# A gated recurrence, worked in units of two chunks of 128 tokens in place of one, ahead of a routed expert layer

## The chip, the cores and the metric

One core of a Trainium2 chip runs the kernel. The metric is the device time of one execution in microseconds, as the median of several runs.

## The reference, cut to what matters

Eight heads of 48 run a gated outer-product recurrence over 768 steps in each of 4 batches; the result, as 3072 tokens of 384, goes through a layer of 8 experts, one expert for each token.

```python
f = 1.0 / (1.0 + np.exp(-f_logit))            # (4, 8, 768, 48)
for t in range(S):
    state = f[:, :, t, :, None] * state + np.einsum('bhd,bhe->bhde', k[:, :, t], v[:, :, t])
    y[:, :, t] = np.einsum('bhd,bhde->bhe', q[:, :, t], state)
x = y.transpose(0, 2, 1, 3).reshape(3072, 384)
logits = x @ w_gate                           # (3072, 8)
expert_idx = np.argmax(logits, axis=1)
gate_w = softmax(logits)[arange, expert_idx]
y[i] = gate_w[i] * (relu(x[i] @ w1[e]) @ w2[e])   # e = expert_idx[i], F = 1024
```

## The kernel before, in words

There are two stages. The first computes the recurrence in 24 chunks of 128 tokens of one batch (`steps`: two batches alternate, then the other two), and routes each token's row to its expert's region of a table `xs` in memory. The second goes over the table in 31 tiles of 128 rows, each with one expert's weights, and scatters the results to the output (from line 513). Between them VectorE works out which tile has which expert, and SyncE writes a tile of padding behind each region (lines 464 to 507). The change is in the first stage alone.

A chunk holds 8 heads as 4 pairs; a head of a pair has 48 of the partitions 0 to 63 or of 64 to 127. So a tile of q, k or f is 128 partitions by 4 pairs by 128 tokens, 512 elements wide. `load` (line 201) fetches it in halves of 96 KB, and v in one transfer, into 5 slots whose unused partitions were filled once (line 194). `prep` (line 213) makes the running product r of 1 + exp(-f) by an Exp, a "plus one" on GpSimd and four scans on VectorE, one for each pair (line 222), capped at 1e19; the decay is exp(-ln r) (lines 224 and 225: Ln and Exp, each with a load of its function table); q is multiplied by the decay, k by r.

`score` (line 231) has the products k by q for each head (16 matmul instructions, as each f32 product takes two), the transposes of k (line 240), a masked copy of the scores by VectorE (line 243) and a copy of the transposed keys by ScalarE (line 245). `rows` (line 270) adds up the rows: "within" (line 274, scores by v) and "before" (line 285, the old state by q), and copies them out (line 294). `update` (line 248) makes the new state: the state products (line 253), a sum and a multiplication by the last decay on VectorE (lines 264 and 265). `gate` (line 297) transposes the rows (line 300, 4 transposes), multiplies them by the gate weights (line 305, 8 thin instructions of 8 columns, with a 128 x 128 weight load each), and copies both out. After each fourth chunk `route` (line 144) chooses the expert, counts by two products with constants (lines 157 and 158), works out each row's position by small VectorE operations, and sends the four chunks by indirect DMAs from GpSimd (line 132).

The loop (line 329) issues these in an order in which the rows of a chunk come one step after its scores. Tile's own scheduler orders the instructions on each engine by priority and readiness. All loads, and one expert's second weights `w2r` in every second step (line 334), go through SyncE's queue. At the end a sum over `rend` (lines 382 to 391) says whether any product reached the cap, in which case another, slow form of the recurrence would run; the data here don't reach it.

## Time and profile before

| | us |
|---|---|
| median of 3 runs (687.83 to 692.0) | 688.04 |
| the profiled execution | 696.35 |
| its span | 694.4 |
| busy: TensorE matmul, its weight loads | 574.7, 457.8 |
| busy: VectorE, ScalarE, GpSimd | 184.4, 164.0, 116.9 |
| mean granted TensorE clock | 0.837 |

The span is the time from the first to the last profiled instruction. Busy times are sums over instructions that don't wait; matmuls are pipelined, so a busy TensorE is not one at its peak. [...] Of all transfers, 100.70 MB in 64164 packets, the mean rate over the span is 145 GB/s.

### The profile page before, as it was taken

What the parts mean: (1) busy time and instruction counts of PE and PEld (TensorE: products, weight loads), DVE (VectorE), ACT (ScalarE), POOL (GpSimd) and SP (SyncE); (2) the same over time, 40 slices, a digit from 0 to 9 for tenths busy, and PEclk for the clock granted to TensorE, in tenths of its full rate; (3) what the DMA queues carried; (4) which work ended last, traced back from release to release, by engine and by line L of the source; (5) the groups of instructions that cost most, each with busy time, mean ns of one, the idle gap of its engine ahead of it and who ended that gap; (6) DMA issues with size and microseconds to landing.
All of it is one profiled execution on the core that took longest, in us unless ns stands there. A gap on an engine that the chain in (4) does not pass through costs nothing.

```text
span 694.4 us, 10369 instructions
## 1 busy us (share of the span) xinstructions
PE 574.7 (83%) x3895; PEld 457.8 (66%) x3895; DVE 184.4 (27%) x504; ACT 164.0 (24%) x231; POOL 116.9 (17%) x185
## 2 busy tenths in 40 slices
PE   0788897696897699506999999999899999999995
PEld 0677776575775577405867777777678677776864
DVE  3555352343253363310111111111111111111120
ACT  4765444536345544101000000000000000000000
POOL 8224213114113123100101010101001010000001
PEclk9988655755565755657999999999999999999998
DMA  7697555653623001055554545453444545363500
GB/s 203 161 268 217 187 133 167 174 158 108 176 62 98 28 1 48 24 194 236 162 182 150 183 131 203 135 206 117 161 169 147 192 134 203 115 215 118 204 32 1
DMA packets 64164, 100.70 MB, mean 145 GB/s; under 512 B 5726, under 2 KB 46721, under 8 KB 64112
## 3 DMA queue, kind: packets, MB, share of 16 engines
q1 hardware_dynamic: 59744, 89.79, 40.8%
q0 software_dynamic: 3520, 9.64, 3.7%
q8 instruction: 33, 0.54, 0.3%
q10 hardware_dynamic: 848, 0.57, 0.3%
q14 instruction: 19, 0.16, 0.1%
HBM read 88.50 MB, written 12.85 MB: 146 GB/s over the span
## 4 chain that ended last, share of the span: by engine, by line
issue 48%; POOL 4%; PE 2%; SPq 1%; DMA 1%; POOLq 0%; DVE 0%
POOL out_dram L132 4%; PE hps L536 1%; DMA xrow<-xs 1%; PE yps L550 1%; SPq L467 1%; SPq L468 0%; POOLq L132 0%; POOLq L594 0%; SPq L517 0%; SPq L516 0%; SPq L519 0%; DVE ysb L554 0%; SPq L521 0%; DVE dst L529 0%
## 5 line engine op out<-in xcount | busy, mean ns | idle before, releaser
L536 PE MATMUL hps<-xT,w1t 128*128 128x128 f32 x1488 | 174.2, 277 | 13.4 <-DVE xT L527 7.6
L536 PEld LDWEIGHTS hps<-xT,w1t 128*128 128x128 f32 x1488 | 171.1, 193 | 21.3 <-DVE xT L527 11.2
L550 PE MATMUL yps<-w2r,hT 128*128 x496 | 171.0, 493 | 13.5 <-DVE hT L546 13.5
L550 PEld LDWEIGHTS yps<-w2r,hT 128*128 128x128 f32 x496 | 90.9, 191 | 77.4 <-DVE hT L546 24.4
L544 ACT ACTIVATE hT<-hps 128x512 f32<-128x512 f32 x31 | 18.5, 597 | 337.4 <-PE hps L536 337.4
L132 POOL DMA_INDIRECT out_dram<-ysb,dst x31 | 30.3, 978 | 361.8 <-DVE ysb L554 326.7
L529 DVE CAST dst<-xrow 128x1 int32<-128x1 f32 x31 | 4.8, 154 | 213.5 <-DMA out_dram<-ysb,dst 193.4
L240 PE MATMUL kp<-fpack,k 128*128 128x128 f32 x96 | 23.6, 389 | 44.4 <-POOL k L228 44.4
L274 PE MATMUL yt<-at,v 128*64 128x128 f32 x384 | 51.2, 382 | 3.8 <-DVE at L243 3.7
L235 PE MATMUL s<-q,k 48*128 48x128 f32 x384 | 48.5, 405 | 3.0 <-DVE q L227 2.9
L240 PEld LDWEIGHTS kp<-fpack,k 128*128 128x128 f32 x96 | 16.0, 203 | 48.9 <-POOL k L228 47.4
L235 PEld LDWEIGHTS s<-q,k 48*128 48x128 f32 x384 | 40.1, 289 | 9.1 <-DVE q L227 5.4
L554 DVE TENSOR_SCALAR ysb<-yps,xrow 128x384 f32<-128x384 f32 x31 | 19.2, 618 | 101.4 <-PE yps L550 101.4
L274 PEld LDWEIGHTS yt<-at,v 128*64 128x64 f32 x384 | 36.4, 193 | 11.4 <-DVE at L243 6.4
L222 DVE TENSOR_TENSOR_SCAN r<-z,fpack 128x128 f32<-128x128 f32 x96 | 35.0, 419 | 24.9 <-POOL z L219 22.9
L243 DVE COPY_PREDICATED at<-mpack,s 128x512 f32<-128x512 uint8 x48 | 33.1, 724 | 30.7 <-PE s L235 30.7
L305 PEld LDWEIGHTS lp<-wg,ys 128*128 128x128 f32 x192 | 33.5, 262 | 4.2 <-issue 2.2
L285 PE MATMUL yt<-q,state 48*48 48x128 f32 x320 | 34.9, 354 | 0.0
L305 PE MATMUL lp<-wg,ys 128*128 128x8 f32 x192 | 33.8, 304 | 0.9 <-ACT ys L294 0.7
L132 POOL DMA_INDIRECT xs<-xr,posi x24 | 24.5, 1022 | 59.3 <-DVE posi L170 34.1
L219 POOL TENSOR_SCALAR z<-z 128x512 f32<-128x512 f32 x24 | 15.7, 655 | 93.2 <-ACT z L218 93.1
L224 ACT ACT_TABLE_LOAD x24 | 30.8, 1283 | 0.4
(86 smaller groups left out, 417.3 us busy)
## 6 DMA issues: line engine op xcount, KB each, us to landing
w1t<-in_moe_w_dram SPq DMA_DIRECT2D x31, 1536.0 KB
w2r<-in_moe_w_dram SPq DMA_DIRECT2D x8, 1536.0 KB
xrow<-xs SPq DMA_DIRECT2D x31, 200.0 KB
v<-in_v_dram SPq DMA_DIRECT2D x24, 256.0 KB
k<-in_kT_dram SPq DMA_DIRECT2D x48, 96.0 KB
f<-in_fT_dram SPq DMA_DIRECT2D x48, 96.0 KB
q<-in_qT_dram SPq DMA_DIRECT2D x48, 96.0 KB
xs<-pad SPq DMA_DIRECT2D x8, 200.0 KB
```

Source lines behind the costliest of these rows:

```text
L132: ins = nc.gpsimd.indirect_dma_start(out=dst, out_offset=bass.IndirectOffsetOnAxis(ap=idx, axis=0), in_=src, in_offset=None, bounds_check= ...
L222: nc.vector.tensor_tensor_scan(r[:, p], z[:, p], const("top"), 1.0, OP.mult, OP.min)
L224: nc.scalar.activation(dec, r, AF.Ln)
L235: nc.tensor.matmul(ps[a][:, p], lhsT=k[r, p], rhs=q[r, p], start=True, stop=True)
L240: nc.tensor.transpose(kp[:, p], k[:, p], ident)
L243: nc.vector.copy_predicated(at[:, :, a], _bc(causal, 1, HP), ps[a])
L274: nc.tensor.matmul(yt[DP * a : DP * a + DP, p], lhsT=vt[:, 2 * p + a], rhs=at[:, p, a], start=p == 0, stop=c == 0, skip_group_check=True,)
L285: nc.tensor.matmul(yt[r, p], lhsT=old[r, p], rhs=q[r, p], start=False, stop=True, skip_group_check=True,)
L305: nc.tensor.matmul(lp, lhsT=ys[:, p], rhs=wg[:, p], start=p == 0, stop=p == HP - 1)
L536: nc.tensor.matmul(hp[:, f, :], lhsT=w1t[:, j, o : o + 128], rhs=xT[:, j, :], start=j == 0, stop=j == KD - 1,)
L550: nc.tensor.matmul(yp, lhsT=hT[:, f, :], rhs=w2r[:, ds(er, 1), f, :], start=f == 0, stop=f == NF - 1)
L554: nc.vector.tensor_scalar(ysb, yp, xt[:, GATE : GATE + 1], None, op0=OP.mult)
```

## The change

A unit is one chunk of two batches: 8 pairs, 1024 elements wide (`SEG` pairs of `C` tokens). The host lays q, k, f and v out by units with the unused partitions filled, so that a unit is loaded by four transfers. Each segment of f gets one more column in front (`CR`), which sets the running product back to 1 (`RESET` there, and 1 in the cap's first column), so that one scan runs over all 8 pairs. All of f, r-logarithm and decay lie in f's own tile. The state's multiplication by the last decay goes to GpSimd. The transposes of the rows and the gate products become one product per pair with a constant of 104 columns: 96 that select the two heads' rows and 8 of gate weights; VectorE adds the four pairs' gate parts (`reduce_sum`). `route` is cut into five calls, of the same operations. The order of the instructions on each of five engines is the order in which the program issues them (`manual_schedule`): pass n of the loop has the scores of unit n, "within" and "before" of unit n - 1, rows and route of unit n - 2, and the front parts of units n + 1 and n + 2. Routes come after units 1, 3, 5, 7 and 9 for two units, and after 10 and 11 for one. The loads of unit n + 3 end the pass; three buffers hold a unit's inputs.

```diff
+NU = B // 2 * NC
+SEG = 2 * HP
+CR = C + 1
+RESET = -30.0
...
+GROUPS = [[u, u + 1] for u in range(0, NU - 2, 2)] + [[NU - 2], [NU - 1]]
+XW = 2 * D + E
...
+    sel = np.zeros((128, HP, XW))
+    for a in range(2):
+        sel[DP * a + np.arange(D), :, D * a + np.arange(D)] = 1.0
+    f["rows"] = sel.reshape(128, HP * XW)
...
+    wx = const("rows").rearrange("p (h w) -> p h w", w=XW)
+    halves = [(a, slice(DP * a, DP * a + D)) for a in range(2)]
+    for a, r in halves:
+        nc.scalar.dma_start(
+            wx[r, :, 2 * D : XW],
+            moe_w_gate.rearrange("(p two d) e -> two d p e", two=2, d=D)[a],
+        )
...
+    class Route:
...
+        def choose(self):
...
+        def count(self, rp):
+            self.rp = rp
+            nc.tensor.matmul(rp[:, 0], lhsT=const("tri"), rhs=self.oh, start=True, stop=True)
+            nc.tensor.matmul(rp[:, 1], lhsT=const("ones"), rhs=self.oh, start=True, stop=True)
+        def place(self):
...
+        def weigh(self):
+            nc.scalar.activation(self.ex, self.ex, AF.Exp)
+        def send(self):
...
+        ld = st.enter_context(tc.tile_pool(name="ld", bufs=3))
...
+        cap = wk.tile([128, SEG, CR], F32, name="cap", bufs=1)
+        nc.vector.memset(cap, RTOP)
+        nc.vector.memset(cap[:, :, 0:1], 1.0)
...
+        def load(u, *names):
+            x = units[u]
+            for n in names:
+                src = {"q": qu, "k": ku, "f": fu, "v": vu}[n]
+                if n == "v":
+                    x[n] = ld.tile([128, 2, H, DP], F32, name=n)
+                else:
+                    x[n] = ld.tile([128, SEG, CR if n == "f" else C], F32, name=n)
+                nc.sync.dma_start(x[n], src[u])
+        def growth(u):
+            f = units[u]["f"]
+            nc.scalar.activation(f, f, AF.Exp, scale=-1.0)
+            nc.gpsimd.tensor_scalar(f, f, 1.0, 1.0, op0=OP.add, op1=OP.mult)
+        def product(u):
+            x = units[u]
+            x["r"] = wk.tile([128, SEG, CR], F32, name="r", bufs=1)
+            nc.vector.tensor_tensor_scan(
+                x["r"].rearrange("p s c -> p (s c)"),
+                x["f"].rearrange("p s c -> p (s c)"),
+                cap.rearrange("p s c -> p (s c)"),
+                1.0,
+                OP.mult,
+                OP.min,
+            )
+        def by_r(u):
+            x = units[u]
+            nc.gpsimd.tensor_tensor(x["k"], x["k"], x["r"][:, :, 1:CR], op=OP.mult)
+            nc.gpsimd.tensor_copy(rend[:, u], x["r"][:, :, C])
+        def log_r(u):
+            x = units[u]
+            nc.scalar.activation(x["f"][:, :, 1:CR], x["r"][:, :, 1:CR], AF.Ln)
+        def decay(u):
+            x = units[u]
+            x["dec"] = x["f"][:, :, 1:CR]
+            nc.scalar.activation(x["dec"], x["dec"], AF.Exp, scale=-1.0)
+        def by_decay(u):
+            x = units[u]
+            nc.vector.tensor_tensor(x["q"], x["q"], x["dec"], op=OP.mult)
+        def heads():
+            return [(p, h, slice(DP * h, DP * h + DP)) for p in range(HP) for h in range(2)]
+        def score(u):
+            x = units[u]
+            x["at"] = scores[u % 2]
+            for a in range(2):
+                ps = pss.tile([128, 2, HP, C], F32, name="s")
+                for p, h, r in heads():
+                    s = HP * a + p
+                    nc.tensor.matmul(
+                        ps[:, h, p], lhsT=x["k"][r, s], rhs=x["q"][r, s], start=True, stop=True
                     )
+                nc.vector.copy_predicated(
+                    x["at"][:, a].rearrange("p h s c -> p (h s) c"),
+                    _bc(causal, 1, SEG),
+                    ps.rearrange("p h s c -> p (h s) c"),
+                )
+        def keys(u):
+            x = units[u]
+            x["kn"] = wk.tile([128, SEG, C], F32, name="kn", bufs=1)
             for a in range(2):
+                kp = pst.tile([128, HP, C], F32, name="kp", **tr)
                 for p in range(HP):
+                    nc.tensor.transpose(kp[:, p], x["k"][:, HP * a + p], ident)
+                nc.scalar.copy(x["kn"][:, HP * a : HP * a + HP], kp)
+        def within(u, a):
+            x = units[u]
+            if a == 0:
+                x["yt"] = psy.tile([128, 2, HP, C], F32, name="yt")
+            for p, h, r in heads():
+                nc.tensor.matmul(
+                    x["yt"][r, a, p],
+                    lhsT=x["v"][:, a, 2 * p + h],
+                    rhs=x["at"][:, a, h, p],
+                    start=p == 0,
+                    stop=x["old"] is None,
+                    skip_group_check=True,
+                )
+        def before(u):
+            x = units[u]
+            if x["old"] is None:
+                return
+            for t in range(2):
+                for p in range(HP):
+                    for a in range(2):
+                        h = a ^ t
+                        r = slice(DP * h, DP * h + D)
                         nc.tensor.matmul(
+                            x["yt"][r, a, p],
+                            lhsT=x["old"][r, HP * a + p],
+                            rhs=x["q"][r, HP * a + p],
                             start=False,
                             stop=True,
                             skip_group_check=True,
                         )
+        def added(u):
+            x = units[u]
+            x["dp"] = pst.tile([128, SEG, D], F32, name="dp", **tr)
+            for a in range(2):
+                for p, h, r in heads():
+                    s = HP * a + p
+                    nc.tensor.matmul(
+                        x["dp"][r, s],
+                        lhsT=x["kn"][:, s, r],
+                        rhs=x["v"][:, a, 2 * p + h, 0:D],
+                        start=s == 0,
+                        stop=True,
+                        skip_group_check=True,
+                    )
+        def update(u):
+            x = units[u]
+            new = wk.tile([128, SEG, D], F32, name="state", bufs=4)
+            last = x["dec"][:, :, C - 1 : C].to_broadcast([128, SEG, D])
+            if x["old"] is None:
+                nc.vector.tensor_copy(new, x["dp"])
+            else:
+                nc.vector.tensor_tensor(new, x["dp"], x["old"], op=OP.add)
+            nc.gpsimd.tensor_tensor(new, new, last, op=OP.mult)
+            states[u % 2] = new
+        def settle(u):
+            x = units[u]
+            x["ys"] = wk.tile([128, 2, HP, C], F32, name="ys", bufs=1)
+            for a in range(2):
+                nc.scalar.copy(x["ys"][:, a], x["yt"][:, a])
...
+        def rows(u):
+            x = units[u]
+            g = next(g for g in GROUPS if u in g)
+            if u == g[0]:
+                n = 2 * len(g)
+                group["xr"] = wk.tile([128, n, ROW], F32, tag="xr", name="xr")
+                group["lg"] = wk.tile([128, n, E], F32, tag="lg", name="lg")
+                nc.gpsimd.memset(group["xr"][:, :, USED:ROW], 0.0)
+            for a in range(2):
+                j = 2 * (u - g[0]) + a
+                xp = pst.tile([128, HP, XW], F32, name="xp", **tr)
+                for p in range(HP):
+                    nc.tensor.matmul(
+                        xp[:, p], lhsT=x["ys"][:, a, p], rhs=wx[:, p], start=True, stop=True
+                    )
+                nc.scalar.copy(
+                    group["xr"][:, j, 0:DM].rearrange("p (h w) -> p h w", h=HP),
+                    xp[:, :, 0 : 2 * D],
                 )
+                nc.vector.reduce_sum(
+                    group["lg"][:, j],
+                    xp[:, :, 2 * D : XW].rearrange("p h e -> p e h"),
+                    axis=AX_X,
                 )
...
+        st.enter_context(tc.manual_schedule(engines=ordered))
+        for u in range(3):
+            load(u, *"fkqv")
+        growth(0)
+        product(0)
+        by_r(0)
+        log_r(0)
+        decay(0)
+        by_decay(0)
+        growth(1)
+        product(1)
+        for n in range(NU + 2):
+            here, back, last = n, n - 1, n - 2
+            rt = None
+            if here < NU:
+                units[here]["old"] = states[here % 2]
+                score(here)
+            if 0 <= last:
+                settle(last)
+            if n + 1 < NU:
+                by_r(n + 1)
+                log_r(n + 1)
+            if 0 <= last:
+                rt = rows(last)
+                if rt:
+                    rt.choose()
+            if here < NU:
+                keys(here)
+            if 0 <= back < NU:
+                within(back, 0)
+            if rt:
+                rt.count(pst.tile([128, 2, rt.n, E], F32, name="rp", **tr))
+            if 0 <= back < NU:
+                within(back, 1)
+            if n + 1 < NU:
+                decay(n + 1)
+                by_decay(n + 1)
+            if rt:
+                rt.place()
+            if here < NU:
+                if here // 2 < NC - 1:
+                    added(here)
+            if n + 2 < NU:
+                growth(n + 2)
+            if rt:
+                rt.weigh()
+            if here < NU and here // 2 < NC - 1:
+                update(here)
+            if rt:
+                rt.send()
+            if n + 2 < NU:
+                product(n + 2)
+            if 0 <= back < NU:
+                before(back)
+            if n + 3 < NU:
+                load(n + 3, *"fkqv")
+            if 1 <= n <= E:
+                e = n - 1
                 nc.sync.dma_start(w2r[:, e], moe_w2[e].rearrange("(f p) d -> p f d", p=128))
...
+    fu = np.full((NU, 128, SEG, CR), RESET, v.dtype)
+    fu[..., 1:] = unit(inputs["f_logit"], 30.0)
```

The fallback and the call of `route` in it use the five calls; nothing from line 464 on is changed.

## Rows read from the trace of the kernel before

**Rows 1.** The page's 40 slices: TensorE's granted clock in tenths.

```profile
PEclk9988655755565755657999999999999999999998
```

**Rows 2.** Stretches of time; the first line names the columns.

```profile
core 0: us, PE busy (x) PEld busy (x) DVE busy (x) ACT busy (x) POOL busy (x), PEclk, DMA share, GB/s
18.70:291.40 272.70, 224.06 (x1811) 185.31 (x1810) 113.32 (x349) 135.68 (x190) 66.24 (x95) 0.65 0.43 125
128.00:132.00 4.00, 4.00 (x58) 3.65 (x54) 1.51 (x3) 0.71 (x2) 0.00 (x0) 1.00 0.67 168
132.00:136.00 4.00, 0.22 (x5) 0.00 (x0) 1.37 (x4) 2.85 (x4) 1.04 (x3) 1.00 1.06 373
136.00:140.00 4.00, 2.64 (x16) 2.24 (x18) 0.69 (x1) 3.21 (x5) 1.59 (x2) 0.60 0.86 178
248.00:260.00 12.00, 12.00 (x79) 9.62 (x80) 6.88 (x31) 4.96 (x9) 2.71 (x4) 0.50 0.01 2
310.00:320.00 10.00, 2.72 (x12) 2.38 (x12) 0.87 (x3) 0.00 (x0) 0.00 (x0) 0.50 1.01 400
```

**Rows 3.** Timeline of TensorE at the full clock: start, length.

```profile
59.12 0.67 PE L253 MATMUL dp<-v,kn 128*64 128x48 f32 x16
61.21 0.63 PE L240 MATMUL kp<-fpack,k 128*128 128x128 f32 x4
...
127.53 1.16 PE L235 MATMUL s<-q,k 48*128 48x128 f32 x16
128.63 0.65 PE L300 MATMUL xtp<-fpack,ys 128*128 128x128 f32 x4
129.12 0.96 PE L305 MATMUL lp<-wg,ys 128*128 128x8 f32 x8
130.00 1.21 PE L274 MATMUL yt<-at,v 128*64 128x128 f32 x16
131.14 1.08 PE L285 MATMUL yt<-q,state 48*48 48x128 f32 x16
```

**Rows 4.** Timeline of TensorE at half the clock.

```profile
265.90 2.08 PE L235 MATMUL s<-q,k 48*128 48x128 f32 x16
```

**Rows 5.** Groups of the first stage: busy us, mean ns, idle before.

```profile
L222 DVE TENSOR_TENSOR_SCAN r<-z,fpack 128x128 f32<-128x128 f32 x96 | 35.0, 419 | 24.9 <-POOL z L219 22.9 <-issue 1.9
L243 DVE COPY_PREDICATED at<-mpack,s 128x512 f32<-128x512 uint8 x48 | 33.1, 724 | 30.7 <-PE s L235 30.7
L224 ACT ACT_TABLE_LOAD x24 | 30.8, 1283 | 0.4
L228 POOL TENSOR_TENSOR k<-k,r 128x512 f32<-128x512 f32 x24 | 30.6, 1274 | 0.0
L132 POOL DMA_INDIRECT xs<-xr,posi x24 | 24.5, 1022 | 59.3 <-DVE posi L170 34.1 <-DVE place L160 19.4 <-issue 5.2
L227 DVE TENSOR_TENSOR q<-q,dec 128x512 f32<-128x512 f32 x24 | 17.5, 731 | 46.2 <-ACT dec L225 46.2
L219 POOL TENSOR_SCALAR z<-z 128x512 f32<-128x512 f32 x24 | 15.7, 655 | 93.2 <-ACT z L218 93.1
L224 ACT ACTIVATE dec<-r 128x512 f32<-128x512 f32 x24 | 15.1, 630 | 24.3 <-DVE r L222 24.1
L265 DVE TENSOR_TENSOR state<-state,dec 128x192 f32<-128x192 f32 x16 | 10.3, 645 | 0.3
```

**Rows 6.** Groups of the same view, narrow operations.

```profile
L173 ACT ACTIVATE ex<-ex 128x32 f32<-128x32 f32 x6 | 1.4, 231 | 3.0 <-DVE ex L172 3.0
L153 DVE TENSOR_TENSOR eq<-lg,mx 128x32 f32<-128x32 f32 x6 | 1.1, 192 | 0.2
```

**Rows 7.** Timeline of VectorE and GpSimd: a state product beside GpSimd's product.

```profile
197.14 1.27 POOL L228 TENSOR_TENSOR k<-k,r 128x512 f32<-128x512 f32 x1
197.20 1.41 DVE L265 TENSOR_TENSOR state<-state,dec 128x192 f32<-128x192 f32 x1
```

**Rows 8.** Timeline of VectorE: the first reader of the packed constants.

```profile
6.15 0.23 DVE L129 COPY base<-fpack 128x8 f32<-128x8 f32 x1 [3.13 <-DMA fpack<-c_fpack]
```

**Rows 9.** Timeline of VectorE: the last routing positions.

```profile
291.19 0.17 DVE L170 CAST posi<-pos 128x4 int32<-128x4 f32 x1
```

More of the change, by code (lines that the diff above doesn't have):

```diff
@@ L87 @@
     vT: bass.AP,
-    v: bass.AP,
+    qu: bass.AP,
+    ku: bass.AP,
+    fu: bass.AP,
+    vu: bass.AP,
     moe_w_gate: bass.AP,
@@ L123 @@
     nc.scalar.dma_start(xs[DUMMY : DUMMY + C], pad)
-    halves = [(a, slice(DP * a, DP * a + D)) for a in range(2)]
-    for a, r in halves:
-        nc.scalar.dma_start(
-            wg[r], moe_w_gate.rearrange("(p two d) e -> two d p e", two=2, d=D)[a]
-        )
     nc.vector.tensor_copy(base[:, 0], const("first"))
@@ L182 @@
+    ordered = {getattr(mybir.EngineType, n) for n in ENGINES}
     with ExitStack() as st:
-        ld = st.enter_context(tc.tile_pool(name="ld", bufs=1))
+        ld = st.enter_context(tc.tile_pool(name="ld", bufs=3))
         wk = st.enter_context(tc.tile_pool(name="wk", bufs=2))
@@ L197 @@
+        nc.vector.memset(cap, RTOP)
+        nc.vector.memset(cap[:, :, 0:1], 1.0)
+        scores = [wk.tile([128, 2, 2, HP, C], F32, name=f"at{i}", bufs=1) for i in range(2)]
         for t in scores:
             nc.vector.memset(t, 0.0)
-        srcs = {"q": qT, "k": kT, "f": fT}
-        def load(n, b, c):
-            cols = slice(c * C, c * C + C)
-            for x in "fkq":
-                for a, r in halves:
-                    nc.sync.dma_start(
-                        slots[x][n % NLD][r],
-                        srcs[x][b, :, :, cols].rearrange("(p two) d s -> two d p s", two=2)[a],
-                    )
-            vt = ld.tile([128, H, DP], F32, tag="v", name="v", bufs=NLD)
-            nc.sync.dma_start(vt, v[b, cols])
-            return vt
@@ L270, in rows @@
[L270 to L284 removed]
+        units = [{} for _ in range(NU)]
@@ L458 @@
                     nc.vector.tensor_copy(lg[:, 0], lp)
-                    rp = gps.tile([128, 2, 1, E], F32, name="grp")
-                    route(gp, rp, lg, [end, end], xr, toks, None)
+                    rt = Route(gp, lg, [end, end], xr, toks, None)
+                    rt.choose()
+                    rt.count(gps.tile([128, 2, 1, E], F32, name="grp"))
+                    rt.place()
+                    rt.weigh()
+                    rt.send()
                     nc.vector.tensor_scalar(toks, toks, float(C), None, op0=OP.add)
@@ L579 @@
         "vT": tokens_last(v),
-        "v": vpad,
+        "qu": unit(inputs["q"], 0.0),
+        "ku": unit(inputs["k"], 0.0),
+        "fu": fu,
+        "vu": vu.reshape(NU, 128, 2, H, DP),
         "moe_w_gate": np.ascontiguousarray(inputs["moe_w_gate"]),
```

255 lines of the change are left out of this document (64 added, 191 removed).

## The prediction, made before the changed kernel ran

> **What bounds the kernel now.** I read the page's slices first, with the clock line beside the engines: the reader is to see the granted clock fall from 9 to between 5 and 7 tenths by the fifth slice, stay there to the 19th, and stand at 9 in the rest [rows 1]. That is a border between two stages. The chain of waits ends in the second stage and says nothing of the first, so I went by stretches of time. From the first score product at 18.7 us to the last routing positions at 291.4 us TensorE is busy 224.06 of 272.70 us, at a mean clock of 0.65; ScalarE is busy 135.68 and VectorE 113.32 us [rows 2]. The second stage (the experts, from about 310 us) is not touched by the change, and what lies between its begin and the last positions is a series of small VectorE and SyncE steps that is not touched either. So the change is worth what it takes off those 291.4 us.
>
> TensorE's 82% there is not 82% of its ability. [...] The clock falls where the engine stands: it had 0.22 us of work between 132 and 136 us, still at 1.00, and in the next 4 us the mean was 0.60 [rows 2]. So there are two levers: less TensorE work, and no long gaps.
>
> **TensorE's work, part by part.** At the full clock a chunk has scores 1.16, the two transposing groups 0.63 (keys) and 0.65 (rows), the thin gate products 0.96, "within" 1.21, "before" 1.08 and the state products 0.67 [rows 3]: 6.36 us, 12.7 for two chunks. The change keeps the first, second, fifth, sixth and seventh in the same number and size (they are only grouped by unit of two chunks), and replaces 4 transposes and 8 thin instructions (1.61 us) by 8 instructions of 104 columns. No row shows these. They cannot take less than the 8 weight loads of the gate products, 0.96 us; as full transposes they would be 8 x 0.163 = 1.3 us. I take 1.0, nearest to the gate's row, since both load 128 x 128 weights. A unit is then 2 x (1.16 + 0.63 + 1.21 + 1.08 + 0.67 + 1.0) = 11.5 us, and 1.2 us less than now, 14 us less over 12 units if all were at full clock. At the lower clock the scores take 2.08 instead of 1.16 us [rows 4], 1.8 times as much, and the unit 21 us. What is left of the gain must come from the clock and from shorter gaps.
>
> **The other engines, per unit.** ScalarE goes by (630 - 231) ns / 480 elements = 0.83 ns an element [rows 5, 6], so 1.06 us for a width of 1024 (bounds: 0.63, the present one, and 1.26, two of these). VectorE's scan in one instruction of 1032 elements is bounded by 1.3 us (an ordinary operation of that width) and 8 x 419 ns = 3.4; the 96 now are busy 35.0 us together, so 8 of them 2.9, and seven starts fewer bring it to 2.5, which I take. The masked copy is 0.72 at 512, and by the slope (731 - 192) / 480 = 1.12 ns becomes 1.3, as does the product q times decay. GpSimd's k times r goes from 1.27 to 2.4 and its "plus one" from 0.66 to 1.1 (upper bounds twice the rows) [rows 5, 6]. Two table loads of 1.28 us go with each unit instead of with each chunk, which takes about 31 us off ScalarE in all.
>
> **One turn of the new loop.** With each engine's order fixed, the longest ring at the full clock runs through VectorE, TensorE, ScalarE and GpSimd: two masked copies 2.6, the first gate sum 0.2 (it frees the buffer of the transposes), four key transposes 0.65, two copies of keys 1.2 (each at most the 0.63 of an activation of that width), table load 1.28, Exp for decay 1.06, Exp for the next growth 1.06, "plus one" 1.1, scan 2.5, and then the next masked copy. That is 11.65 us and ten hand-overs of some 0.07, 12.3 us. q times decay (1.3) and the state's sum (0.5) lie beside Exp and "plus one". In every second turn a route lies in it as well: behind the decay come q times decay 1.3, 12 small operations 2.0 (0.19 for the first row of that kind [rows 6], some overlapping), the sum 0.5, three more 0.6 and the scan 2.5, 6.9 in place of 4.7 us, so 14.5. Four scatters of 1.02 us and GpSimd's start of each [rows 5] fit beside it: GpSimd then has about 10 us of work in 14.5. If this cover were gone, the 5 us of scatters would hold back the next k times r and so the scores.
>
> The state's second multiplication moves from VectorE to GpSimd. The trace shows what two-operand work on both does: beside k times r the 192-wide state product on VectorE took 1.41 us, while the mean over all 16, some of them disturbed too, is 0.65 [rows 5, 7]. Its new place is just ahead of the scan, so I add 0.3 us a turn (bounds 0 and 1.0, the length of that product).
>
> ScalarE's first work in a turn, the two copies of rows, waits for the end of "before"; behind it in its queue stand Ln, the copies of rows and keys and the decay, 5 us of work, which the scores (2.3) and row products (2.0) on TensorE nearly cover. TensorE needs 11.5 to 12 us of such a turn, and ScalarE 9. All three are near to one another, and TensorE has one wait in a turn, ahead of the key transposes, until the masked copies are through: for about 1 us in a plain turn, 3 us in one with a route. A gap of 3 us is near to that of 132 to 136 us, after which the clock fell. I take it that it falls once in two turns and is back by the end of the row products: keys and within then cost 3 us more. Two turns are 12.3 + 14.5 + 0.6 + 3 = 30.4 us, 15.2 each.
>
> **The transfers.** By its shapes a unit loads 2.1 MB instead of 1.7, in rows of 4 KB where they were 512 bytes; with one expert's weights (1.57 MB) and the scatters (0.4 MB) eight turns move 4.1 MB each. In the one stretch where nothing held the queues back they moved 400 GB/s at a share of 1.01 [rows 2]; by that a turn's bytes take 10 us, beside 15. The new load of q waits for "before" of three units earlier, and the v, w2r and next f behind it on SP's queue wait with it; q, v, w2r and f are 3.1 MB, 8 us at that rate and some 3 of delay, 11 in all; f is wanted after about 15. I count nothing, and if it is late, the growth is what waits. The 15 memsets of slots and the 24 small copies of token numbers that go count for nothing: they are GpSimd's, which has 66.24 us of work in the stage's 272.70 [rows 2].
>
> **Begin and end.** The first reader of the packed constants starts at 6.15 us [rows 8]. The gate weights are now written into that pack, so ScalarE's queue holds two transfers that wait for it. With some 2 us for the larger pack and these two issues (an estimate) its first Exp starts no sooner than 8.3 + 1.28. From there: Exp 1.06, 1.1, scan 2.5, Ln 1.06, load and Exp 2.3, the second unit's Exp, "plus one" and scan 4.7: first masked copy at 22.3 us (the first scores are at 18.7 now, so nothing is won here). Turns 0 and 1 have no rows to wait for: 9.3 each. Turns 2 to 9: 8 x 15.2 = 122. Turns 10 and 11 lack the front part, 10 each; 12 and 13 drain: 9 and 7 to the last positions. Sum: 22.3 + 18.6 + 122 + 36 = 199 us, where it is 291.4 now [rows 9]. That is 92 us less. The profiled execution took 696.35 us (span 694.4), which gives 604; it is 8.3 us above the median of the runs, 688.04, and the forecast for the median is 688 - 92 = 596 us. If the clock never falls, two turns are 27.4 and the stage 12 us shorter: 584.
>
> [...] The rows show that a gap precedes the fall [rows 2]; none shows a stretch of transposes alone. [...]
>
> **The rivals.** First, the lower clock throughout. For: the stage is so for most of its time today, with TensorE busy and the clock at 0.50 for 12 us on end [rows 2]. Against: within and before now lie in runs of 32 each, where each had 16, and the full clock after 128 us held over just such a run of both [rows 3]. Price: eight turns of 21, turns 1, 10 and 11 at 13, 18.5 and 18.5, the drain 21: 22.3 + 9.3 + 13 + 168 + 37 + 21 = 271, a gain of 20, 668 us.
>
> Second, the clock falls in each turn, not in each second one. For: the gap of a plain turn, 1 us, grows with every wait that I have not counted. Against: no row shows a fall behind a gap that short. Price: 3 us more in four turns, 12 in all, 608 us.
>
> Third, on the other side: the transfers become the bound. Place: SP's queue in turns 1 to 8, where the load of q holds back w2r and the next f. At the mean rate of the whole span, 145 GB/s on the page, 4.1 MB take 28 us a turn and the stage 22.3 + 18.6 + 224 + 36 = 301: 698 us, slower. It decides from a turn of 26.8 us, that is from 153 GB/s downward. Against it: the 400 GB/s.
>
> Fourth, the fixed order buys nothing: each engine waits for the one before it at the present 23 us a unit, and the time stays at 688.
>
> **How the numbers follow.** Clock falling once in two turns, 596: 0.42. Never, 584: 0.18. Every turn, 608: 0.20. Lower clock throughout, 668: 0.11. Transfers: 0.05. Nothing: 0.04. The first three hold 0.80, and with the unknown prices (scan 1.3 to 3.4, the collision up to 1.0, each over 10 turns, so about 12 us down and 15 up) they reach from 570 to about 625; taking in most of the way to the fourth, 650, leaves out less than 2 in 10. About 1% is what a measurement of this kernel can tell from no change. The first four cases are faster by more: 0.91, of which I leave 0.90. Within 1%: 0.04. Slower: the third rival and what I have not seen, 0.06.
>
> **What would show it.** Right: last positions near 200 us; granted clock of the stage at 0.75 or more; TensorE's longest wait ahead of the key transposes; scans at about 2.5 us; 24 fewer table loads. Wrong: clock near 0.5 with TensorE busy all through (first rival), growth waiting for f (third), or a begin much later than 22 us.

## The result, and the profile after

The changed kernel takes 596.55 us (median of 4 runs, 593.54 to 600.35), the kernel before 690.02 in the runs beside it (687.83 to 697.25). The ratio is 0.863, 95% interval 0.855 to 0.872; all ratios leave out runs more than 1.5% above the fastest of their kernel. The forecast was 596, range 570 to 650.

The page of the changed kernel: the span, the busy times and TensorE's clock by slices, as in [rows 1].

```profile
span 591.8 us, 9687 instructions
## 1 busy us (share of the span) xinstructions
PE 485.2 (82%) x3803; PEld 396.2 (67%) x3803; DVE 177.0 (30%) x373; ACT 126.0 (21%) x172; POOL 115.2 (19%) x121
...
PEclk9888969979898559999999999999999999999998
```

Of the 5s, 6s and 7s of the first third a 6 and a 7 are left; the two 5s now stand in the steps between the stages (slices 14 and 15, from 192 us). Stretches of the changed kernel, columns as in [rows 2] (PEclk is a share of the full clock): the two stages, then turns 3, 4, 8 and 9 of the loop, each from one masked copy to the next.

```profile
14.30:187.70 173.40, 136.10 (x1724) 124.32 (x1724) 104.23 (x217) 97.82 (x133) 78.48 (x79) 0.88 0.62 222
187.70:591.80 404.10, 349.11 (x2079) 271.86 (x2079) 64.73 (x150) 19.80 (x32) 32.27 (x33) 0.95 0.45 154
50.77:65.16 14.39, 12.15 (x146) 11.02 (x145) 10.98 (x30) 8.39 (x12) 5.60 (x6) 0.76 0.38 138
65.16:83.00 17.84, 13.10 (x168) 12.30 (x167) 7.34 (x8) 8.88 (x12) 9.27 (x9) 0.87 1.00 359
125.20:137.80 12.60, 10.03 (x136) 9.46 (x136) 7.26 (x8) 7.99 (x11) 8.39 (x10) 0.73 0.75 267
137.80:154.03 16.23, 12.67 (x176) 11.40 (x173) 10.85 (x29) 9.38 (x13) 6.27 (x5) 1.00 0.94 333
```

From the last positions on, the span has 404.1 us left, where it had 694.4 - 291.4 = 403.0. So the whole gain is in the first stage: TensorE's busy time there fell from 224 to 136 us, by less work and a faster clock together, and the clock rose from 0.65 to 0.88. But plain turn 4, at a clock of 0.87, is longer than plain turn 8 at 0.73, and turn 9, at 1.00, is longer than turn 3 at 0.76 (both carry a route). So in the new loop something other than the clock makes the longest turns.

The groups of the changed kernel that answer to [rows 5]:

```profile
L258 DVE TENSOR_TENSOR_SCAN r<-f,cap 128x1032 f32<-128x1032 f32 x12 | 32.4, 2703 | 10.1 <-POOL f L252 10.1
L269 POOL TENSOR_TENSOR k<-k,r 128x1024 f32<-128x1024 f32 x12 | 26.2, 2187 | 18.6 <-DVE r L258 14.0
L274 ACT ACT_TABLE_LOAD x12 | 15.4, 1283 | 2.3 <-DMA fpack<-c_fpack 2.1
L279 ACT ACT_TABLE_LOAD x12 | 15.4, 1283 | 0.2
```

The 48 table loads of the stage are 24, and the sizes came out near the estimates (masked copy 1.29 us, in the last row below; k times r 2.19). The timeline of the changed kernel shows the ring of turn 3:

```profile
50.77 2.47 DVE L298 COPY_PREDICATED at<-mpack,s 128x1024 f32<-128x1024 uint8 x2
53.14 0.27 DVE L404 TENSOR_REDUCE lg<-xp 128x8 f32<-128x32 f32 x2
53.37 1.09 PE L310 MATMUL kp<-fpack,k 128*128 128x128 f32 x8 [2.24 <-DVE lg L404]
54.11 1.07 ACT L311 COPY kn<-kp 128x512 f32<-128x512 f32 x2 [1.43 <-PE kp L310]
55.20 1.28 ACT L279 ACT_TABLE_LOAD   x1
56.50 1.06 ACT L279 ACTIVATE f<-f 128x1024 f32<-128x1024 f32 x1
57.59 1.23 DVE L283 TENSOR_TENSOR q<-q,f 128x1024 f32<-128x1024 f32 x1 [2.96 <-ACT f L279]
...
62.97 2.28 DVE L258 TENSOR_TENSOR_SCAN r<-f,cap 128x1032 f32<-128x1032 f32 x1
65.16 1.29 DVE L298 COPY_PREDICATED at<-mpack,s 128x1024 f32<-128x1024 uint8 x1
```

Follow the starts down: each begins about where the one before it ends, from VectorE to TensorE, ScalarE and back, as the prediction walked it; the dots stand mainly for the small operations of the route on VectorE. Two waits tell what it missed. The ends of TensorE's and ScalarE's idle times in the changed kernel, from the begin to 200 us (us in total, times, longest):

```profile
PE kp L310 <- DVE lg L404: 20.8, 10, 3.9
ACT f L251 <- DMA f<-in_fu_dram: 14.9, 5, 6.0
```

The first is the wait ahead of the key transposes that was forecast. The second was not forecast as a cost: ScalarE's Exp for the growth stands until f has landed. The DMA engines in 40 slices from 48 to 82 us, and the issues on SP's queue (start, length) in the same stretch, show why.

```profile
DMA  9999999810000000005677989999999999999999
```

```profile
49.09 0.43 SPq L246 DMA_DIRECT2D k<-in_ku_dram  x1
63.04 0.33 SPq L246 DMA_DIRECT2D q<-in_qu_dram  x1
63.41 1.89 SPq L246 DMA_DIRECT2D v<-in_vu_dram  x1
65.34 0.43 SPq L481 DMA_DIRECT2D w2r<-in_moe_w_dram  x1
65.87 0.52 SPq L246 DMA_DIRECT2D f<-in_fu_dram  x1
```

```profile
77.91 1.06 ACT L251 ACTIVATE f<-f 128x1032 f32<-128x1032 f32 x1 [5.97 <-DMA f<-in_fu_dram]
```

From 49.5 to 63.04 us SP's queue holds a load of q until "before" of the unit that used its buffer is through, and the DMA engines stand still behind it for some 7 us (a slice is 0.85 us). Then q, v, w2r and f run together at a share of 1.00, and ScalarE's Exp for turn 4 waits 5.97 us for f (last row, the timeline of ScalarE).

### The profile page after: what moved, and what is told of

It reads as the page before. It is cut to its first block, busy times and chain, and to the rows that moved or that the text cites. A ratio compares the mean times of both kernels' runs of the same rounds, so it can differ in the third digit from the quotient of the medians.

```text
span 591.8 us, 9687 instructions
## 1 busy us (share of the span) xinstructions
PE 485.2 (82%) x3803; PEld 396.2 (67%) x3803; DVE 177.0 (30%) x373; ACT 126.0 (21%) x172; POOL 115.2 (19%) x121
## 4 chain that ended last, share of the span: by engine, by line
issue 56%; POOL 5%; PE 2%; SPq 2%; DMA 1%; POOLq 0%; DVE 0%
POOL out_dram L149 5%; PE hps L644 1%; DMA xrow<-xs 1%; PE yps L658 1%; SPq L575 1%; SPq L576 1%; SPq L625 0%; POOLq L149 0%; SPq L624 0%; POOLq L715 0%; SPq L627 0%; SPq L629 0%; DVE ysb L662 0%; DVE more L588 0%; DVE nt L592 0%
## 5 line engine op out<-in xcount | busy, mean ns | idle before, releaser
L295 PE MATMUL s<-q,k 64*128 64x128 f32 x384 | 28.1, 303 | 19.6 <-DVE q L283 19.6
L295 PEld LDWEIGHTS s<-q,k 64*128 64x128 f32 x384 | 25.8, 211 | 21.3 <-issue 20.6
L258 DVE TENSOR_TENSOR_SCAN r<-f,cap 128x1032 f32<-128x1032 f32 x12 | 32.4, 2703 | 10.1 <-POOL f L252 10.1
L310 PE MATMUL kp<-fpack,k 128*128 128x128 f32 x96 | 18.4, 351 | 20.8 <-DVE lg L404 20.8
L319 PE MATMUL yt<-at,v 128*64 128x128 f32 x384 | 32.0, 328 | 0.0
L397 PE MATMUL xp<-fpack,ys 128*128 128x104 f32 x192 | 26.1, 292 | 7.2 <-ACT ys L380 7.2
L298 DVE COPY_PREDICATED at<-mpack,s 128x1024 f32<-128x1024 uint8 x24 | 29.6, 1287 | 1.6 <-PE s L295 1.6
L397 PEld LDWEIGHTS xp<-fpack,ys 128*128 128x128 f32 x192 | 24.0, 203 | 9.0 <-ACT ys L380 8.1
L269 POOL TENSOR_TENSOR k<-k,r 128x1024 f32<-128x1024 f32 x12 | 26.2, 2187 | 18.6 <-DVE r L258 14.0
L310 PEld LDWEIGHTS kp<-fpack,k 128*128 128x128 f32 x96 | 14.4, 180 | 23.2 <-DVE lg L404 22.6
L633 PE MATMUL etp<-fpack,xrow 128*128 128x128 f32 x93 | 13.2, 278 | 20.4 <-issue 20.4
L283 DVE TENSOR_TENSOR q<-q,f 128x1024 f32<-128x1024 f32 x12 | 15.0, 1247 | 44.7 <-ACT f L279 44.7
```

The lines of the kernel that those rows point to most:

```text
L258: nc.vector.tensor_tensor_scan(x["r"].rearrange("p s c -> p (s c)"), x["f"].rearrange("p s c -> p (s c)"), cap.rearrange("p s c -> p (s c) ...
L269: nc.gpsimd.tensor_tensor(x["k"], x["k"], x["r"][:, :, 1:CR], op=OP.mult)
L295: nc.tensor.matmul(ps[:, h, p], lhsT=x["k"][r, s], rhs=x["q"][r, s], start=True, stop=True)
L298: nc.vector.copy_predicated(x["at"][:, a].rearrange("p h s c -> p (h s) c"), _bc(causal, 1, SEG), ps.rearrange("p h s c -> p (h s) c"),)
L310: nc.tensor.transpose(kp[:, p], x["k"][:, HP * a + p], ident)
L319: nc.tensor.matmul(x["yt"][r, a, p], lhsT=x["v"][:, a, 2 * p + h], rhs=x["at"][:, a, h, p], start=p == 0, stop=x["old"] is None, skip_grou ...
```

## The experiments

Three theories of the 93 us were to be told apart: **units** (fewer table loads and starts, and a short ring), **the clock** (TensorE faster because it no longer falls) and **the fixed order**. Each kernel is the changed one with the edit shown, or one of the experiments so named. The median of the kernel before was 690.0 to 697.6 beside the different kernels, so ratios to it are compared, and medians only of kernels that ran side by side.

**The fixed order alone.**

```diff
-        st.enter_context(tc.manual_schedule(engines=ordered))
```

> Only the fixed order is taken out; Tile's scheduler orders the engines by priority and readiness as in the kernel before. If the fixed order is a main part of the gain, the recurrence again ends after 230 us or later and the time is 635 us or more. If units of 1024 columns and the single product are what pays, it stays within 590 to 610 us.

Measured 595.04 us, ratio 0.858 (0.850 to 0.866): no difference from the changed kernel. With Tile's own scheduler back, the last positions come at 194.2 us in place of 187.5, at a mean clock of 0.938 over the span (0.932): the turns are cut otherwise (10.8 to 19.3 us). In these two traces the fixed order is thus some 7 us ahead in the stage, but what follows the last positions takes 4.3 us longer with it (404.1 against 399.8). On the whole kernel it bought nothing that can be measured.

**The key transposes first in a pass**, to shorten TensorE's wait and so the fall of the clock.

```diff
+            if here < NU:
+                keys(here)
             if n + 1 < NU:
                 by_r(n + 1)
...
-            if here < NU:
-                keys(here)
```

> Only the place of the key transposes and their two copies moves: ahead of Ln and of the row products. Ring theory (a turn is masked copies, gate sum, key transposes, key copies, table load, two Exps, plus one, scan): the masked copies drop out of the ring, a plain turn falls from 12.6 to about 11.5 us and one with a route from 14.3 to about 13, 8 to 14 us in all: 583 to 589 us. Clock theory (the turn is TensorE's work over the granted clock): the wait only moves to the row products, same time as the changed kernel, 594 to 600 us.

Measured 597.45 us, ratio 0.862 (0.854 to 0.869): nothing. In its trace turns 2 to 9 take 111.9 us in place of 115.9, but turns 0 and 1 take 24.8 in place of 20.8, which eats that up. ScalarE still waited five times for f, 15.6 us together, so the result does not tell the two theories apart.

**The loads by need.** Pass n fetches q and v of unit n + 2 and f and k of n + 3, all ahead of w2r. SP's queue then holds q, v, f, k, w2r behind one another, where it held q, v, w2r, f, k.

```diff
-        for u in range(3):
+        for u in range(2):
             load(u, *"fkqv")
+        load(2, *"fk")
...
+            if n + 2 < NU:
+                load(n + 2, *"qv")
             if n + 3 < NU:
-                load(n + 3, *"fkqv")
+                load(n + 3, *"fk")
```

> q and v are loaded one pass later, f and k of the next unit stand ahead of the expert's weights on SyncE's queue. Transfer theory: ScalarE's waits for f (14.9 us in five places, 6.0 in the longest) go, and 8 to 13 us with them: 584 to 589 us. Ring theory alone: the waits lie beside other waits, less than 4 us: 593 to 600 us.

Measured 584.59 us, ratio 0.844 (0.836 to 0.851); repeated without an edit:

> The kernel of e_loads once more, as the control of the three below: 582 to 588 us.

586.25 us, 0.846 (0.842 to 0.850). Beside the changed kernel's 0.863 that is some 12 us less. ScalarE's waits for f sank from 14.9 to 0.9 us, and the last positions came at 177.7 us. So the late f cost the changed kernel about 12 us, which the prediction had counted as nothing. The load of q still waits for its buffer here; what changed is that f does not stand behind w2r too (SP's queue at the end of turn 3):

```profile
60.77 0.33 SPq L246 DMA_DIRECT2D q<-in_qu_dram  x1
...
62.74 0.38 SPq L246 DMA_DIRECT2D f<-in_fu_dram  x1
...
63.63 0.43 SPq L484 DMA_DIRECT2D w2r<-in_moe_w_dram  x1
```

ScalarE's Exp on this f starts at 69.68 us and waits for nothing.

This kernel also tells what a fall of the clock costs, since its turns of one kind differ in little else. Its four turns with a route:

```profile
48.50:62.99 14.49, 12.25 (x147) 11.00 (x146) 10.97 (x29) 8.59 (x12) 5.60 (x6) 0.76 0.53 193
75.28:89.66 14.38, 11.89 (x143) 10.82 (x143) 10.97 (x29) 8.39 (x12) 5.73 (x6) 0.76 0.75 279
101.87:116.25 14.38, 10.57 (x158) 9.54 (x156) 10.97 (x29) 8.65 (x12) 5.74 (x6) 1.00 0.97 355
128.85:143.26 14.41, 12.37 (x172) 11.29 (x172) 11.00 (x30) 9.15 (x13) 5.74 (x6) 1.00 0.91 312
```

Two turns with a mean clock of 0.76 and two with 1.00 have one length, 14.4 us. A plain turn with a fall took 12.60, two without 12.21 and 12.29 (and 11.85 the first, which has no scatters beside it). A fall costs 0 to 0.4 us here, and where it comes decides: in the two turns at 0.76 the clock fell late in the key transposes or after them, in the plain turn of 12.60 it caught them. In the changed kernel it caught them in turns 2, 5 and 8. In turn 5 they took 1.97 us, where turn 3 has 1.09:

```profile
85.60 1.97 PE L310 MATMUL kp<-fpack,k 128*128 128x128 f32 x8 [2.36 <-DVE lg L404]
```

Turns 2 and 5 took 12.62 and 15.15 us there, against 11.85 and 14.38 here. So in these two traces a fall cost nothing where TensorE's slow work lay beside the ring, and 0.4 to 0.8 us where it caught the key transposes, which lie on it.

**Two products again in place of the one of 104 columns**: transposes and thin gate products as before, in the fixed order.

```diff
-                xp = pst.tile([128, HP, XW], F32, name="xp", **tr)
+                xp = pst.tile([128, HP, 2, DP], F32, name="xp", **tr)
...
+                    nc.tensor.transpose(
...
+                lp = pst.tile([128, E], F32, name="lp", **tr)
...
+                        rhs=wx[:, p, 2 * D : XW],
...
+                nc.vector.tensor_copy(group["lg"][:, j], lp)
```

> The single product of 104 columns is undone: 4 transposes and 4 gate products of 8 columns per chunk, as in the kernel before, in the same fixed order. If TensorE's work sets the turn: 1.2 us a unit at full clock, more at half, 14 to 25 us in all: 610 to 622 us. If the ring sets it: TensorE's wait ahead of the key transposes takes most of it up, 0 to 6 us: 596 to 603 us.

Measured 616.5 us, ratio 0.885 (0.875 to 0.896): 0.022 of 694 us above the changed kernel by the ratios, 15 us, and 19 to 21 us above the free order and the keys first, which ran beside it and take the changed kernel's time. That is in the range of the first theory. But two of the waits of its first 200 us, with the columns as above, show that it is not TensorE's work alone (the profiled run was its longest, 620.28 us):

```profile
DVE lg L413 <- PE lp L406: 21.9, 12, 2.8
...
PEld xp L397 <- ACT xr L400: 17.3, 9, 3.7
```

The gate parts take two more tiles a unit from the two buffers that rows, keys and state products share, so TensorE waits for ScalarE's copy of rows, and VectorE's queue for the thin products. How much of it is work and how much these buffers was not told apart.

**The one product alone, in the kernel before** (one chunk of one batch, Tile's order): its 104 columns, the constant and the sum, nothing else.

```diff
-                    lp, lhsT=ys[:, p], rhs=wg[:, p], start=p == 0, stop=p == HP - 1
+                    xp[:, p], lhsT=ys[:, p], rhs=wx[:, p], start=True, stop=True
```

> The kernel before with one part of the change alone: one product of 104 columns per pair in place of the transposes and the gate products. If the stage before is TensorE at the lower clock, 24 chunks save 1.0 to 1.2 us each at that clock, and more where the clock comes back: 20 to 40 us, 650 to 670 us. If it is bound by waits, under 7 us: 683 us or more.

Measured 674.92 us, ratio 0.983 (0.967 to 0.999): some 12 us less, with an interval from 1 to 23, and between the two ranges that were expected. The stretch that answers to the first of [rows 2]:

```profile
18.70:273.70 255.00, 190.25 (x1714) 158.22 (x1714) 116.23 (x349) 135.56 (x190) 65.56 (x95) 0.73 0.48 135
```

TensorE's busy time in the stage fell by 34 us and its clock rose from 0.65 to 0.73; the stage got 272.7 - 255.0 = 17.7 us shorter in these two traces, of which that before is of a run longer than its median. By the ratio this part alone is about an eighth of the 93 us.

**Four table loads in a unit again**, on top of the loads by need: Ln and Exp in two halves by turns.

```diff
-            nc.scalar.activation(x["f"][:, :, 1:CR], x["r"][:, :, 1:CR], AF.Ln)
+            f, r = x["f"][:, :, 1:CR], x["r"][:, :, 1:CR]
+            nc.scalar.activation(f[:, 0:HP], r[:, 0:HP], AF.Ln)
+            nc.scalar.activation(f[:, 0:HP], f[:, 0:HP], AF.Exp, scale=-1.0)
+            nc.scalar.activation(f[:, HP:SEG], r[:, HP:SEG], AF.Ln)
...
+            half = x["dec"][:, HP:SEG]
+            nc.scalar.activation(half, half, AF.Exp, scale=-1.0)
```

> e_loads with Ln and Exp of a unit in two halves by turns, so four table loads a unit instead of two (as many as one for each chunk): 3.4 us more on ScalarE between the scan and the copies of the rows, 0.4 less behind the key copies. Ring theory: 2 to 2.5 us a turn, 20 to 25 us: 604 to 610 us. If TensorE or the transfers set the turn: under 5 us, 584 to 590 us.

Measured 619.09 us, ratio 0.900 (0.889 to 0.911): 0.054 of 694 us, 37, above the loads by need by the ratio of their repeat, and 34.6 above the keys first with these loads (below), which ran beside it. That is more than the ring theory's 20 to 25. Turns 2 to 9 of the loads by need, and under them the same eight turns with the tables:

```profile
36.65:143.26 106.61, 87.80 (x1204) 80.56 (x1202) 73.02 (x142) 69.09 (x92) 53.87 (x53) 0.90 0.85 298
```

```profile
45.70:176.84 131.14, 100.86 (x1202) 92.78 (x1200) 73.09 (x141) 92.59 (x124) 57.76 (x53) 0.80 0.67 236
```

ScalarE is busy 23.5 us more in these eight turns: 16 loads of 1.283 us are 20.5 of it; the rest is near what 16 more activations would add, by an estimate from the means of the kernel before and the changed one: two of 512 columns take 2 x 0.63 us, one of 1024 takes 1.06, 0.2 more for each. The length of the turns grew by 24.5, so nearly all of it lies on the ring. (A fall of the clock caught the key transposes in six of the eight turns, in the loads by need in one, so some of the 24.5, at most 4, may be that.) This is the largest single part that was undone. No kernel here has fewer than two loads a unit, one for Ln and one for Exp, so what the last 24 of the changed kernel (30.8 us of ScalarE) cost was not shown.

**Eight scans in place of one.**

```diff
-            nc.vector.tensor_tensor_scan(
-                x["r"].rearrange("p s c -> p (s c)"),
...
+            for s in range(SEG):
+                nc.vector.tensor_tensor_scan(
+                    x["r"][:, s], x["f"][:, s], cap[:, s], 1.0, OP.mult, OP.min
+                )
```

> e_loads with eight scans of 129 elements in place of one of 1032. By the present 419 ns each they overlap to 2.7 to 2.9 us instead of 2.3, in the ring in each of ten turns: 4 to 8 us more than the control by the ring theory. If VectorE has room there: under 2 us.

Measured 597.01 us, ratio 0.862 (0.858 to 0.865), 10.8 us over the loads by need that ran beside it, more than the 4 to 8 expected. The scans themselves are the smaller part. One of 129 columns takes 0.397 us, but the next starts 0.32 us after it, and eight are through in 2.61 us where nothing disturbs them; one of 1032 columns takes 2.28. That is 0.33 us a unit, 4 in twelve. Most of the rest is a table load. With one scan ScalarE loads Ln's table while the scan runs; with eight the load itself stood until they were through (ScalarE in turn 4 into turn 5, the loads by need first, the eight scans second):

```profile
72.51 1.28 ACT L274 ACT_TABLE_LOAD   x1
75.39 1.06 ACT L274 ACTIVATE f<-r 128x1024 f32<-128x1024 f32 x1 [1.60 <-DVE r L258]
```

```profile
84.51 1.28 ACT L270 ACT_TABLE_LOAD   x1 [1.43 <-DVE r L259]
```

Turns 5 and 9, where no fall caught the key transposes, took 15.28 us against 14.38 and 14.41.

**The state's multiplication back on VectorE.**

```diff
-            nc.gpsimd.tensor_tensor(new, new, last, op=OP.mult)
+            nc.vector.tensor_tensor(new, new, last, op=OP.mult)
```

> e_loads with the state's multiplication by the last decay back on VectorE. Collision theory: the scan in plain turns takes 2.3 instead of 2.95 us, 3 us less over five turns, and turns with a route take 0.5 more each, 2.5 us in all: within 2 us of the control. If the moved work itself mattered, 5 us more.

Measured 583.79 us, ratio 0.840 (0.837 to 0.844), against 0.846 (0.842 to 0.850): 2.5 us less, not told from noise. The trace is clear: every scan is then 2.28 to 2.31 us. With the product on GpSimd the scan of a plain turn stretches beside it, as in this pair of the changed kernel (GpSimd's row from its own timeline):

```profile
47.84 0.84 POOL L373 TENSOR_TENSOR state<-state,f 128x384 f32<-128x384 f32 x1
47.91 2.94 DVE L258 TENSOR_TENSOR_SCAN r<-f,cap 128x1032 f32<-128x1032 f32 x1 [0.48 <-POOL f L252]
```

**Keys first, with the loads by need**, from pass 2 on.

> The loads of e_loads, and from pass 2 on the key transposes ahead of Ln and of the row products. If the ring through the masked copies sets the turn once f is in time: a plain turn stays at 12.2 us (Exp, plus one and scan remain), one with a route falls from 14.4 to about 12.8, 6 to 10 us in all against e_loads: 575 to 579 us. If TensorE at its granted clock sets it: no gain, 583 to 587 us.

Measured 584.48 us, ratio 0.852 (0.841 to 0.864). Eight turns are 100.5 us in its trace in place of 106.6, the last positions at 174.2 in place of 177.7; but that trace is of the fastest of its four runs (579.53 us), and neither the median nor the ratio shows a gain.

**Work for TensorE in the gap**, so that the clock doesn't fall: the second batch's row products three times more in passes with a route.

```diff
-                for p in range(HP):
+                again = 4 if a and u == g[-1] else 1
+                for p in [p for _ in range(again) for p in range(HP)]:
```

> e_loads with the second batch's row products repeated three times more in each pass that has a route (24 instructions, some 3 us, same result), in the gap after which the clock fell. Clock theory (each fall costs 3 us of the ring): the clock stays up, 5 falls fewer, 10 to 15 us less: 570 to 575 us. Ring theory: the clock stays up and nothing is gained, since TensorE at half the clock was beside the ring: 582 to 588 us.

Measured 600.58 us, ratio 0.873 (0.862 to 0.884). It missed its aim: the copies of rows waited for the added products, so these lay on the ring (turns with a route of 15.1 to 17.5 us). The clock stayed up in those four turns, and stood at half in five other stretches. It says nothing on the clock's worth.

**Three edits together**: loads by need, keys first from pass 2, the state's multiplication on VectorE in passes without a route.

```diff
-            nc.gpsimd.tensor_tensor(new, new, last, op=OP.mult)
+            eng = nc.gpsimd if routed else nc.vector
+            eng.tensor_tensor(new, new, last, op=OP.mult)
```

> The loads of e_loads, the key transposes early from pass 2 on as in e_keys_loads, and the state's multiplication on VectorE in turns without a route, on GpSimd in the others. Ring theory: 5 us from the shorter turns with a route and 2 to 3 from the collision, 575 to 581 us, below the control by 5 to 9. If TensorE sets the turn: as the control.

Measured 582.27 us, ratio 0.841 (0.837 to 0.845). It is faster than both kernels, the changed one by some 15 us. Over the loads by need alone, which ran beside it, its 4 us are within overlapping intervals, and the 575 to 581 of the ring theory were missed.

## Why the prediction was right, and where it was lucky

**Place and ring: right.** The gain is in the first stage alone, and the new turn is the ring that was walked. Forecast 12.3 + 0.3 for a plain turn; the changed kernel has 12.60 to 12.84 where f is not over 1 us late, the loads by need 11.9 to 12.6. With a route 14.5 + 0.3 against 14.2 to 15.15 in the changed kernel (turn 9 apart, where f came 4.3 us late) and 14.4 to 14.5 in the loads by need. In the loads by need, the eight turns take 106.6 us where the ring without falls gives 4 x (12.6 + 14.8) = 109.6. The row products were put at 1.0 a chunk and took 2.03 for two (16 instructions at the full clock); the scan at 2.5, and is 2.28 alone; collision 0.3 a turn, in fact 0.66 in a plain turn (2.94 less 2.28), and 0 or 0.54 in one with a route. No row shows the 0.07 us of a hand-over, which was the author's estimate; in turn 3 of the changed kernel q times decay starts 0.03 us behind the end of ScalarE's Exp, and "plus one" 0.09 behind its own. The end was 33.7 us against 36.

**Falls of the clock: the count about right, the price wrong.** The step "keys and within then cost 3 us more" put 12 us into eight turns. TensorE's instructions do take longer after the gap: in turn 3 two groups of 16 "within" read 1.97 and 1.98 us, where [rows 3] has 1.21. But "within" lies beside ScalarE's table load and Exp, which the ring goes through. Only the key transposes lie on it: at half the clock they take 0.9 us more, and the turn 0.4 to 0.8. So the measured price of a fall is 0 to 0.8 us, some 2 us in turns 2 to 9 of the changed kernel (turns 2, 5 and 8) in place of 12. The error is that of adding an engine's slower work to a path that had left this engine. It also brings the second rival (608) and the never-fall case (584) within a few us of one another. Nor did the clock fall in each turn, as the second rival had it. It stood at half in 7 stretches of the changed kernel's first 12 turns and in 5 of the loads by need, in turns of both kinds. In turns 4, 7 and 9 of the changed kernel, where TensorE had waited 0.5 to 1.5 us ahead of them, the transposes ran at the full clock (1.09 us for eight) and no fall followed them (that of turn 4, at 78.3 us, came in a wait of 3.93 us ahead of the row products); it fell in the three turns with a wait of over 3 us ahead of the transposes (3.3 to 3.9: turns 6, 8 and 10), and in turns 2 and 3 with one of 2.24. No run here takes the gap and the transposes apart.

**Transfers: wrong.** "I count nothing" was the step. The bytes fit, as argued: 359 GB/s in turn 4. What failed is the order within the queue. The prediction saw that v, w2r and f wait behind q, and gave it "11 in all" for f wanted "after about 15". But q could not start at the begin of the turn: it waited for "before", which in a turn with a route ends near the turn's end (63.04 in a turn from 50.77 to 65.16), so f, behind q, v and w2r, was issued at 65.87 and used at 77.91. Price about 12 us. The third rival had the right place, but no turn came near its 28 us; the longest was 17.84.

**Begin: 5 us too late.** Forecast 22.3 us to the first masked copy, measured 17.36. No row shows the 2 us for the larger pack, an estimate; its first reader starts at 7.08 us, 0.93 later than before, and the first Exp, which was to start no sooner than 9.58, started at 4.79. The gate weights' transfers into the pack were issued at 7.08, behind this Exp. ScalarE's next table load stood 2.13 us behind them, but the Ln that it is for waited for the first scan all the same, so they held next to nothing back (the timeline of ScalarE in the changed kernel):

```profile
4.79 1.06 ACT L251 ACTIVATE f<-f 128x1032 f32<-128x1032 f32 x1 [1.36 <-DMA f<-in_fu_dram]
7.08 0.87 ACTq L139 DMA_DIRECT2D fpack<-in_moe_w_gate_dram  x2
7.98 1.28 ACT L274 ACT_TABLE_LOAD   x1 [2.13 <-DMA fpack<-c_fpack]
9.51 1.06 ACT L274 ACTIVATE f<-r 128x1024 f32<-128x1024 f32 x1 [0.24 <-DVE r L258]
```

**So the sum is nearer than its terms.** By terms, forecast and measured: begin 22.3 and 17.4, turns 0 and 1 18.6 and 20.8, turns 2 to 9 122 and 115.9, end 36 and 33.7; 199 and 187.7. Within turns 2 to 9 falls counted some 10 too much, late loads some 8 too little (115.9 against 106.6 in the loads by need, less the falls of turns 2 and 5), and the ring itself some 3 too much. The stage gained 291.4 - 187.7 = 103.7 us in the traces, some 11 more than forecast, while the medians differ by 93.5: the profiled run before (696.35) stands 6 us above the median of its kernel in this comparison, that of the changed kernel (593.54) 3 us below its own. An error in the stage and one in the reference point met at 596. That the forecast meets the median to 1 us is luck.

**Two levers, and what was shown of them.** The prediction put "less TensorE work, and no long gaps" first. Undone one at a time, the halved table loads are worth some 35 us; the one product 15 to 21 in the new loop, and some 12 when it is put alone into the kernel before; the long scan some 4; the fixed order and the state's move nothing that can be measured. These don't add up in a strict sense, since each was taken from another ring, and they leave some 35 of the 93 us without an experiment of their own: the unit of two chunks, with fewer starts and hand-overs, was never undone as a whole, and the clock was never varied alone. Among runs of the kernel before the time goes with the mean clock (681.85 us at 0.875, 688.23 at 0.858, 697.59 at 0.840), so the clock may well count there, but that shows no cause. What the higher clock by itself is worth stays open. The order of the fourth rival did buy nothing, but its 688 fell with its premise that the order was all there was to gain.

## What to carry to other kernels

When work moves into a pipeline of several engines, first find the ring that each turn must go through, and charge a slower instruction only if it lies on the ring: half the clock on TensorE cost nothing here except on the key transposes (0.4 to 0.8 us a turn), while the added table loads counted nearly in full (24.5 us in eight turns). When an edit that undoes a part costs more than that part's own time, look for what else it moved: eight scans cost 4 us themselves and put a table load on the ring. In a DMA queue that one engine issues in order, look at what stands behind a load that waits for its buffer, and put what is wanted first ahead of what can wait: the same bytes in another order were worth 12 us. And when a forecast comes out to the microsecond, check its terms against the trace all the same.

## What the runs showed of the hardware that was not expected

Two small VectorE operations of a route took longer beside GpSimd's. In turn 3 of the changed kernel, timelines of VectorE and GpSimd, VectorE's first:

```profile
58.73 1.02 DVE L193 COPY place<-base 128x8 f32<-128x8 f32 x1
...
62.01 0.82 DVE L211 TENSOR_SCALAR su<-su 128x4 f32<-128x4 f32 x1
```

```profile
58.60 1.13 POOL L252 TENSOR_SCALAR f<-f 128x1032 f32<-128x1032 f32 x1 [5.30 <-ACT f L251]
61.97 0.84 POOL L373 TENSOR_TENSOR state<-state,f 128x384 f32<-128x384 f32 x1 [2.24 <-DVE su L210]
```

A copy of 8 elements and an operation on 4 take 1.02 and 0.82 us; both end just as GpSimd's instruction ends (59.75 and 59.73, 62.83 and 62.81). Without a GpSimd instruction beside them they take 0.17: the copy in turn 7 of the same kernel, where f and with it GpSimd's "plus one" came late, and the operation on 4 in turn 3 of the run with the state's multiplication on VectorE:

```profile
118.97 0.17 DVE L193 COPY place<-base 128x8 f32<-128x8 f32 x1
```

```profile
60.64 0.17 DVE L211 TENSOR_SCALAR su<-su 128x4 f32<-128x4 f32 x1
```

The prediction priced the collision of two large operations; in a turn with a route it is small ones, on VectorE's part of the ring, that lose some 0.8 and 0.65 us. What holds the small ones until GpSimd's are through, no run shows.
